# Attention on one Trainium2 core: chunk ends of the product with V, and where one query group is transposed

## The chip, the cores and the metric

The kernel runs on one core of one Trainium2 chip. The metric is the device time of one execution in microseconds (us). A core has five engines that each work through a queue of their own in order: TensorE (PE in the rows, its weight loads PEld), VectorE (DVE), ScalarE (ACT), GpSimd (POOL) and SyncE (SP, which here issues DMA transfers). They wait for one another by semaphores.

## The reference, cut to what matters

The program is an attention, then a dense layer, then a routed layer. The change touches the attention alone:

```
B, H, S, D = 4, 8, 1152, 64
q_pool = q.reshape(B, H, S // 2, 2, D).mean(axis=3)      # 576 queries a head
scores = np.matmul(q_pool, k.transpose(0, 1, 3, 2)) / np.sqrt(D)
attn = np.exp(scores - np.max(scores, axis=-1, keepdims=True))
attn = attn / (np.sum(attn, axis=-1, keepdims=True) + 1e-09)
out = np.matmul(attn, v)                                  # then the two layers
```

All arithmetic is 32 bit; the matmuls take each operand as a high part in a rounded format and a low part with the rest, so most products are issued twice or more.

## The kernel before

**Tiles and steps.** `attention` (L24) works on 16 pairs of heads. A pair has 2 × 576 = 1152 queries, which are nine tiles of 128; tile 4 holds the end of the first head and the start of the second. The main loop (L280) has one step `g` for each tile: `i, t = divmod(g, 9)` is the pair and the tile. A step works on two tiles at once: it finishes tile `g` and prepares tile `g+2`. The order of the work within a step is written out in `SEQ` (L17), and every engine gets its instructions in that order:

- `q1`, `q0` (`qk`, L158): scores of tile `g+2`, as products of the transposed queries `qa`/`qb` and the transposed keys `kst`; six matmuls of 384 columns (two into `Sb`, four into `Sa`), for tile 4 twice as many. `Sa` has one buffer in PSUM, so its next scores wait for ScalarE's exponential of the last ones.
- `m1`, `m0`, `bias` (L174 to L179): row maxima on VectorE; `e0`, `e1` (`exp`, L180): exponentials on ScalarE, into `P`.
- `t0`, `t1`, `t2` (`tp`, L212): nine transposes on TensorE of tile `g`'s `P`, three to a PSUM tile `T`; `c0` to `c2` (`evH`, L226) copy them out on ScalarE as high parts `PH`, `l0` to `l2` (`evL`, L228) subtract on VectorE for the low parts `PL`. `T` is a ring of three buffers, and everything else that is transposed takes its buffers from the same ring, in order.
- `av`, `aw` (`takeav`, L275): matmuls of the product with V, from a list that is filled chunk by chunk. `AVN[t]` is how many a step takes, the larger half at `av`, the rest at `aw`.
- `pool`, `scl`: GpSimd's work (high and low parts of keys, values and queries, from the table `POOL`; the scaling of finished outputs by `rB`, L244).
- `prep`: transposes of later pairs' queries and keys, from the table `PREP`: `T0` to `T2` are keys (`top`, L123), `q0` to `q2` query groups (`qop`, L132). Each is three transposes into a `T` and one or two copies by ScalarE; a query group then also issues two DMA transfers `qb<-qa` on SP (L145, L146).
- `inv`: reciprocals of the row sums (`invT`, L191, one transpose into a `T` at t=3 and t=7), their way through DRAM, and the load of `rB` (`invB`, L199, on SP at t=0 and t=5); `st`: stores of outputs.
- `sum`, `dec`: sums of rows, and from step 70 on single instructions that decode the next layer's weights.

**Chunks.** The product with V is made in four chunks a pair (`av_ops`, L230) of 256, 320, 320 and 256 queries. Each has 18 matmuls (nine key tiles, high and low) that add up in `O`, for which PSUM has one buffer. The last one of a chunk is followed by ScalarE's copy `xo<-O` (L242), and the first of the next chunk waits for that copy. `DONE` (L274) says after which step a chunk's matmuls are put on the list: `{1:[0],4:[1],6:[2],8:[3]}`, step and chunk. With the counts of before, a pair's chunk 2 begins at t=7 after one matmul that ends chunk 1, and chunk 3 begins at t=0 of the next pair after four matmuls that end chunk 2; chunks 0 and 3 end with the last matmul of t=4 and of t=2.

Of the kernel before, what the change touches and what calls it, by code (L numbers as in the profile page):

```python
# [14 lines left out]


SEQ='q1 q0 m1 sum dec t0 c0 m0 pool scl t1 c1 bias l0 t2 av c2 l1 e0 e1 l2 aw prep inv st'.split()  # L17
AVN=(9,3,10,7,11,7,10,7,8)
PREP={0:((1,'T0'),),2:((1,'T1'),),3:((1,'T2'),),5:((1,'q2'),),7:((2,'q0'),),8:((2,'q1'),)}
POOL={0:((0,'vH1'),(0,'vL1')),1:((1,'H0'),(1,'L0')),3:((1,'H1'),(1,'L1')),4:((1,'H2'),(1,'L2')),5:((2,'qadd'),),6:((2,'qH'),(2,'qL')),8:((1,'vH0'),(1,'vL0'))}  # L20
SPQ={4:((1,'D0'),),7:((1,'D1'),)}
SCALE=(7,8,11,12)
# [1 line left out]
def attention(tc, q, k, v, xS, rS, ident, pairs=None, extra=(), start=lambda: None):  # L24
# [5 lines left out]
    with ctx:  # L30
# [18 lines left out]
        def load(i,what="qkv",eng=None):  # L49
            if i>=len(pairs): return  # L50
            b,hp=pairs[i]; h0=2*hp
            d=D_.setdefault(i,dict(ks={},vs={},kst={}))
            for w in what:
                if w=='q':
                    t=d['qn']=ld.tile([128,KT,2,D],F32,name="qn")
                    (eng or nc.sync).dma_start(out=t,in_=q[b,h0:h0+2].rearrange("h (s r) d -> (h s) (r d)",r=2).rearrange("(t p) x -> p t x",p=128))
                else:
                    t=d[w+'n']=ld.tile([128,2,KT,D],F32,name=w+"n")
                    (eng or nc.sync).dma_start(out=t,in_={'k':k,'v':v}[w][b,h0:h0+2].rearrange("h (p t) d -> p h t d",p=128))
# [98 lines left out]
        def qk(g,n):  # L158
            i,t=divmod(g,9); d=D_[i]
            if g not in st: new(g)  # L160
            A=QA[i%2]; Bq=QB[i%2]
            if t==4: L=[(512,0),(640,1)]
            else: L=[(128*t,0)] if t<4 else [(128*t+128,1)]
            ops=[(w[:,c:c+128],h) for c,h in L for w in (A,Bq)]
            if n==0:
                o=psS.tile([128,2,512],F32,name="Sa"); st[g]['S'][0]=o[:,:,0:384]
                outs=[(o[:,j,0:384],j) for j in range(2)]
            else:
                o=psU.tile([128,384],F32,name="Sb"); st[g]['S'][1]=o
                outs=[(o,2)]  # L170
            for o,j in outs:
                for x,(w,h) in enumerate(ops):
                    nc.tensor.matmul(o,w,d['kst'][h][:,j*384:(j+1)*384],start=(x==0),stop=(x==len(ops)-1))  # L173
        def smax(g,n):  # L174
            s=st[g]
            nc.vector.tensor_reduce(out=s['nm'][:,n:n+1],in_=s['S'][n],axis=AX.XY if n==0 else AX.X,op=ALU.max,negate=True)  # L176
        def bias(g):
            nm=st[g]['nm']
            nc.vector.tensor_reduce(out=st[g]['bs'],in_=nm,axis=AX.X,op=ALU.min)  # L179
        def exp(g,n):  # L180
            s=st[g]; P=s['P']
            o=P[:,0:768].rearrange("p (c x) -> p c x",x=384) if n==0 else P[:,768:1152]
            nc.scalar.activation(out=o,in_=s['S'][n],func=AF.Exp,bias=s['bs'],scale=1.0,accum_out=s['su'][:,n:n+1])  # L183
# [3 lines left out]
        def ssum(i,h):  # L187
            a,b=TS[h]; r=inv[i,h]=sm.tile([128,2,5],F32,name="rc",bufs=2)
            nc.vector.tensor_reduce(out=r[:,0,0:b-a],in_=sus[:,i%2,a:b],axis=AX.X,op=ALU.add)
            nc.vector.reciprocal(out=r[:,1,0:b-a],in_=r[:,0,0:b-a])  # L190
        def invT(i,h):  # L191
            a,b=TS[h]; bb,hp=pairs[i]; n=b-a
            T=psT.tile([128,384],F32,name="T",tag="T")
            nc.tensor.transpose(T[0:n,0:128],inv.pop((i,h))[:,1,0:n],ident)
            o=sm.tile([5,128],F32,name="ro",bufs=1)
            nc.scalar.copy(out=o[0:n],in_=T[0:n,0:128])
            flat=rS[bb][hp:hp+1].rearrange("o h s -> (o h s)")
            nc.sync.dma_start(out=flat[128*a:128*b].rearrange("(t p) -> t p",p=128),in_=o[0:n])
        def invB(i,h):  # L199
            bb,hp=pairs[i]  # L200
            flat=rS[bb][hp:hp+1].rearrange("o h s -> (o h s)")
            r=rB[i,h]=sm.tile([128,576],F32,name="rB",bufs=2)
            nc.sync.dma_start(out=r,in_=flat[576*h:576*h+576].partition_broadcast(128))
# [8 lines left out]
        def tp(g,j):  # L212
            T=psT.tile([128,384],F32,name="T",tag="T"); P=st[g]['P']
            for n in range(3):
                kt=3*j+n
                nc.tensor.transpose(T[:,n*128:(n+1)*128],P[:,kt*128:(kt+1)*128],ident)  # L216
            st[g][j]=T
# [8 lines left out]
        def evH(g,j):  # L226
            for H,L,src in parts(g,j): nc.scalar.copy(out=H,in_=src)  # L227
        def evL(g,j):  # L228
            for H,L,src in reversed(list(parts(g,j))): nc.vector.tensor_tensor(out=L,in0=src,in1=H.bitcast(F32),op=ALU.subtract)  # L229
# [24 lines left out]
        def take(l,n=1):  # L254
            for _ in range(n):
                if l: l.pop(0)()
        ops={}
        def do(i,*names):

            if i>=N: return  # L260
            if i not in ops: ops[i]=pool_ops(i,i==0)|prep_ops(i)
            for n in names:
                o=ops[i].pop(n,None)
                if o: o()
# [10 lines left out]
        def takeav(n):  # L275
            while avq and n>0:
                avq[0].pop(0)(); n-=1
                if not avq[0]: avq.pop(0)
        stores=[]; sums={}
        for g in range(NG+4):  # L280
            i,t=divmod(g,9)
            if g<NG:
                if t==2 and i>0: load(i+1,'v')
                if t==2: load(i+2,'q')
                if t==5: load(i+2,'k')
            f2=g+2<NG; f0=g<NG
            if not f0:
                while avq: takeav(99)
            for op in SEQ:
                a=op[:-1]; n=op[-1]  # L290
                if op=='scl':
                    if g in at: x,y=at.pop(g); x(); stores.append((g,y))
                elif op=='st':
                    while stores and (stores[0][0]<g or not f0): stores.pop(0)[1]()
                elif op=='inv':
                    if f0 and t in (3,7): invT(i,t//4)
                    if t==5 and f0: invB(i,0)
                    if t==0 and i>0: invB(i-1,1)
                    for di,x in SPQ.get(t,()): f0 and do(i+di,x)
                    if g in (0,2): do(1,'q0' if g==0 else 'q1')  # L300
                elif not f0: pass
                elif a=='q': f2 and qk(g+2,int(n))
                elif a=='m': f2 and smax(g+2,int(n))
                elif a=='e': f2 and exp(g+2,int(n))
                elif op=='bias': f2 and bias(g+2)
                elif a=='t': tp(g,int(n))
                elif a=='c': evH(g,int(n))
                elif op in ('av','aw'): takeav((AVN[t]+(op=='av'))//2)
                elif a=='l': evL(g,int(n))
                elif op=='sum':  # L310
                    if t in (3,7): ssum(i,t//4)
                elif op in ('pool','prep'):
                    for di,n in (POOL if op=='pool' else PREP).get(t,()): do(i+di,n)
                elif op=='dec':
                    want=NX*max(0,g-70)//max(1,NG-74); take(extra,want-(NX-len(extra)))
                else: raise Exception(op)
            if f0:
                for c in DONE.get(t,[]): avq.append(av_ops(i,c))
# [552 lines left out]
def full(tc,q,k,v,w_in,w_out,emb,tau,w1,w2,out,dbg=None):  # L871
# [7 lines left out]
    with contextlib.ExitStack() as ctx:  # L879
# [7 lines left out]
        with tc.manual_schedule():  # L887
# [17 lines left out]
            for n in range(4):  # L905
                pre+=ops[n][1]
                if n+2<4: pre.append(ops[n+2][0])
            for n in range(2): pre+=[lambda n=n: X.load(n)]+X.split_ops(n)
            attention(tc,q,k,v,xS,rS,ident,extra=pre,start=norms)
            wp2=pool(right,"w2",side="right")  # L910
            W0.append(wp2.tile([128,2,1024],F32R,name="W2",tag="W2"))
# [109 lines left out]
```

## Time and profile before

| | us |
|---|---|
| median of 3 runs | 1350.07 (1348.87 to 1350.55) |
| profiled execution, its own time | 1348.71 |
| span of that execution, first to last instruction | 1346.6 |
| TensorE busy (its weight loads) | 1229.3 (1084.1) |
| VectorE, ScalarE, GpSimd busy | 1095.5, 892.2, 635.6 |

Times in the rows are us from the start of the span. A row of a timeline has the start, the duration, the engine, the source line, the operation, what is written and read, and how many instructions were merged (x9); in square brackets how long the engine had been idle before it, and what it waited for. The ends of matmuls are modelled, since they are pipelined: the distance of two starts says what one costs.

### The profile page before, as it was taken

What the parts mean: (1) busy time and instruction counts of PE and PEld (TensorE: products, weight loads), DVE (VectorE), ACT (ScalarE), POOL (GpSimd) and SP (SyncE); (2) the same over time, 40 slices, a digit from 0 to 9 for tenths busy, and PEclk for the clock granted to TensorE, in tenths of its full rate; (3) what the DMA queues carried; (4) which work ended last, traced back from release to release, by engine and by line L of the source; (5) the groups of instructions that cost most, each with busy time, mean ns of one, the idle gap of its engine ahead of it and who ended that gap; (6) DMA issues with size and microseconds to landing.
All of it is one profiled execution on the core that took longest, in us unless ns stands there. A gap on an engine that the chain in (4) does not pass through costs nothing. (4 is left out here: it accounts for less than half of the span.)

```text
span 1346.6 us, 22379 instructions
## 1 busy us (share of the span) xinstructions
PE 1229.3 (91%) x7341; PEld 1084.1 (81%) x7341; DVE 1095.5 (81%) x1970; ACT 892.2 (66%) x2059; POOL 635.6 (47%) x567
## 2 busy tenths in 40 slices
PE   5999999999999999977768989899999999999997
PEld 4888888888888888865657879797989887788885
DVE  5788888888888888789997697848485889998894
ACT  6888888888888888744445645454556657576772
POOL 3444444444555555256667443424342435455852
PEclk9999999999999999989898999999999999999999
DMA  5554555556555575244331311010101323258710
GB/s 165 141 143 127 128 154 138 139 142 168 152 151 137 132 187 140 58 139 117 109 102 48 109 41 36 25 40 16 40 17 47 138 72 138 94 191 328 278 36 22
DMA packets 119624, 154.34 MB, mean 115 GB/s; under 512 B 12135, under 2 KB 93943, under 8 KB 115152
## 3 DMA queue, kind: packets, MB, share of 16 engines
q1 hardware_dynamic: 115232, 140.93, 36.7%
q0 software_dynamic: 3696, 11.34, 2.4%
q8 instruction: 60, 0.98, 0.3%
q10 hardware_dynamic: 576, 0.59, 0.1%
q14 instruction: 60, 0.49, 0.1%
HBM read 155.48 MB, written 20.28 MB: 131 GB/s over the span
## 5 line engine op out<-in xcount | busy, mean ns | idle before, releaser
L430 PE MATMUL h<-xH,W 128*128 128x384 f32 (+1 forms) x896 | 229.0, 327 | 51.5 <-ACT yt L439 37.5
L227 ACT CAST PH<-T 128x384 fp32r<-128x384 f32 (+1 forms) x480 | 185.7, 460 | 84.7 <-PE T L216 84.6
L229 DVE TENSOR_TENSOR PL<-T,PH 128x384 fp32r<-128x384 f32 (+1 forms) x480 | 217.4, 508 | 6.4 <-ACT PH L227 6.3
L430 PEld LDWEIGHTS h<-xH,W 128*128 128x128 f32 x896 | 161.8, 195 | 72.3 <-ACT yt L439 48.3
L453 POOL TENSOR_TENSOR gL<-et,gH 128x384 fp32r<-128x384 f32 (+1 forms) x112 | 120.1, 1072 | 197.7 <-ACT gH L452 170.1
L818 DVE TENSOR_TENSOR W<-sg,W 128x2048 fp32r<-128x2048 f32 (+1 forms) x84 | 193.9, 2341 | 14.1 <-POOL W L816 7.2
L435 ACT ACTIVATE em<-h 128x384 f32<-128x384 f32 (+1 forms) x112 | 49.8, 445 | 224.4 <-DVE et L444 149.5
L239 PE MATMUL O<-PH,vs 128*128 128x256 f32 (+1 forms) x576 | 166.3, 311 | 17.9 <-ACT xo L242 17.9
L176 DVE TENSOR_REDUCE nm<-Sa 128x1 f32<-128x768 f32 x144 | 136.8, 950 | 40.6 <-PE Sa L173 35.1
L216 PE MATMUL T<-ident,P 128*128 128x128 f32 x1296 | 164.8, 272 | 0.0
L239 PE MATMUL O<-PL,vs 128*128 128x256 f32 (+1 forms) x576 | 161.9, 303 | 0.0
L216 PEld LDWEIGHTS T<-ident,P 128*128 128x128 f32 x1296 | 150.1, 140 | 5.2
L430 PE MATMUL h<-xL,W 128*128 128x384 f32 (+1 forms) x448 | 144.0, 321 | 0.7 <-DVE xL L385 0.7
L444 DVE SCALAR_TENSOR_TENSOR et<-em,et 128x384 f32<-128x384 f32 (+1 forms) x112 | 69.5, 621 | 84.4 <-ACT em L441 82.8
L183 ACT ACTIVATE P<-Sa,bs 128x768 f32<-128x768 f32 x144 | 133.6, 928 | 4.1 <-DVE bs L179 3.9
L173 PE MATMUL Sa<-kst,qa 128*128 128x384 f32 x320 | 114.5, 358 | 16.7 <-ACT P L183 14.8
L239 PEld LDWEIGHTS O<-PH,vs 128*128 128x128 f32 x576 | 108.6, 189 | 25.6 <-ACT xo L242 23.9
L817 ACT CAST W<-sg 128x2048 fp32r<-128x2048 f32 (+1 forms) x63 | 114.2, 1835 | 15.0 <-DMA sg<-moe_w 15.0
L461 PE MATMUL y<-W,gH 128*128 128x512 f32 x288 | 115.7, 402 | 0.0
L176 DVE TENSOR_REDUCE nm<-Sb 128x1 f32<-128x384 f32 x144 | 79.8, 554 | 42.6 <-PE Sb L173 41.7
L462 PE MATMUL y<-W,gH 128*128 128x512 f32 x288 | 113.8, 395 | 0.0
L239 PEld LDWEIGHTS O<-PL,vs 128*128 128x128 f32 x576 | 108.8, 189 | 0.0
(298 smaller groups left out, 2940.9 us busy)
## 6 DMA issues: line engine op xcount, KB each, us to landing
sg<-moe_w SPq DMA_DIRECT2D x80, 1024.0 KB
qn<-q SPq DMA_DIRECT2D x16, 576.0 KB
kn<-k SPq DMA_DIRECT2D x16, 576.0 KB
rB<-rS SPq DMA_DIRECT2D x32, 288.0 KB
vn<-v SPq DMA_DIRECT2D x15, 576.0 KB
dx<-moe_w_in SPq DMA_DIRECT2D x16, 512.0 KB
dx<-moe_w_out SPq DMA_DIRECT2D x16, 512.0 KB
qb<-qa SPq DMA_DIRECT2D x64, 96.0 KB
```

Source lines behind the costliest of these rows:

```text
L173: nc.tensor.matmul(o,w,d['kst'][h][:,j*384:(j+1)*384],start=(x==0),stop=(x==len(ops)-1))
L176: nc.vector.tensor_reduce(out=s['nm'][:,n:n+1],in_=s['S'][n],axis=AX.XY if n==0 else AX.X,op=ALU.max,negate=True)
L183: nc.scalar.activation(out=o,in_=s['S'][n],func=AF.Exp,bias=s['bs'],scale=1.0,accum_out=s['su'][:,n:n+1])
L216: nc.tensor.transpose(T[:,n*128:(n+1)*128],P[:,kt*128:(kt+1)*128],ident)
L227: for H,L,src in parts(g,j): nc.scalar.copy(out=H,in_=src)
L229: for H,L,src in reversed(list(parts(g,j))): nc.vector.tensor_tensor(out=L,in0=src,in1=H.bitcast(F32),op=ALU.subtract)
L239: nc.tensor.matmul(O[0][:,:n],vs[:,kt].rearrange("p a d -> p (a d)"),R[:,kt,:n],start=first,stop=last)
L430: nc.tensor.matmul(h[:,:N],a,b[:,k,:N],start=(n==0),stop=(n==11)); n+=1
L453: nc.gpsimd.tensor_tensor(out=gL[:,:N],in0=t_,in1=gH[:,:N].bitcast(F32),op=ALU.subtract)
L461: nc.tensor.matmul(y,gH[:,sl],wH,start=(f==0),stop=False)
L817: else: nc.scalar.copy(out=H[:,q],in_=s[:,q])
L818: (nc.gpsimd if (w,j,h) in self.pool_L else nc.vector).tensor_tensor(out=L[:,q],in0=s[:,q],in1=H[:,q].bitcast(F32),op=ALU.subtract)
```

## The change

Three tables or lines of the order are changed, and no instruction is added or dropped.

- `AVN`, the matmuls of the product with V in each step, from (9,3,10,7,11,7,10,7,8) to (6,3,9,7,11,8,10,8,10). The sum stays 72. Chunks 1 and 2 now end with the last matmul of t=6 and of t=8; chunks 0 and 3 end where they did.
- `PREP`: the second query group `q1` was transposed at t=8 for the pair after the next; it now is at t=0 for the next pair, which is one step later, ahead of the first keys `T0` of the same step.
- The start-up: pair 1's `q1` was made at step 2 and now comes with the others of t=0, in step 0.

```diff
-AVN=(9,3,10,7,11,7,10,7,8)
-PREP={0:((1,'T0'),),2:((1,'T1'),),3:((1,'T2'),),5:((1,'q2'),),7:((2,'q0'),),8:((2,'q1'),)}
+AVN=(6,3,9,7,11,8,10,8,10)
+PREP={0:((1,'q1'),(1,'T0')),2:((1,'T1'),),3:((1,'T2'),),5:((1,'q2'),),7:((2,'q0'),)}
...
-                    if g in (0,2): do(1,'q0' if g==0 else 'q1')
+                    if g==0: do(1,'q0')
```

## Rows read from the trace of the kernel before

**Rows 1.** The page: the span in 40 slices, busy tenths and granted clock.

```profile
PE   5999999999999999977768989899999999999997
PEclk9999999999999999989898999999999999999999
```

**Rows 2.** Timeline, TensorE, pairs 6 and 7: the first transposes of steps.

```profile
216.93 1.14 PE L216 MATMUL T<-ident,P 128*128 128x128 f32 x9
...
220.45 1.15 PE L216 MATMUL T<-ident,P 128*128 128x128 f32 x9
...
224.77 1.15 PE L216 MATMUL T<-ident,P 128*128 128x128 f32 x9
...
228.32 1.14 PE L216 MATMUL T<-ident,P 128*128 128x128 f32 x9
...
232.68 1.14 PE L216 MATMUL T<-ident,P 128*128 128x128 f32 x9
...
236.88 1.14 PE L216 MATMUL T<-ident,P 128*128 128x128 f32 x9
...
262.56 1.14 PE L216 MATMUL T<-ident,P 128*128 128x128 f32 x9
```

**Rows 3.** Waits, first 572 us: who waited for whom, us in total, times, longest.

```profile
PE O L239 <- ACT xo L242: 17.9, 32, 0.7
```

**Rows 4.** Timeline, all engines, step t=1 of pair 7.

```profile
233.21 1.25 ACT L227 CAST PH<-T 128x384 fp32r<-128x384 f32 x3 [0.45 <-PE T L216]
...
234.32 0.93 ACT L183 ACTIVATE P<-Sa,bs 128x768 f32<-128x768 f32 x1
...
235.39 0.44 PE L173 MATMUL Sa<-kst,qa 128*128 128x384 f32 x1 [0.51 <-ACT P L183]
```

**Rows 5.** Timeline, TensorE, steps t=6 and t=7 of pair 6.

```profile
218.06 0.31 PE L239 MATMUL O<-PH,vs 128*128 128x320 f32 x1
...
219.38 0.34 PE L173 MATMUL Sb<-kst,qa 128*128 128x384 f32 x1
...
221.35 0.39 PE L239 MATMUL O<-PL,vs 128*128 128x320 f32 x1
222.29 0.41 PE L239 MATMUL O<-PH,vs 128*128 128x320 f32 x1 [0.56 <-ACT xo L242]
...
223.28 0.49 PE L136 MATMUL T<-ident,qsp 128*128 128x128 f32 x3
```

**Rows 6.** Timeline, VectorE, step t=0 of pair 7.

```profile
229.58 1.01 DVE L229 TENSOR_TENSOR PL<-T,PH 128x384 fp32r<-128x384 f32 x2
```

**Rows 7.** Timeline, all engines, the first step of the main loop.

```profile
24.05 1.48 DVE L229 TENSOR_TENSOR PL<-T,PH 128x384 fp32r<-128x384 f32 x3
...
25.18 0.31 PEld L136 LDWEIGHTS T<-ident,qsp 128*128 128x128 f32 x3 [0.22 <-issue]
...
26.61 1.15 PE L216 MATMUL T<-ident,P 128*128 128x128 f32 x9
```

**Rows 8.** Timeline, ScalarE, ends of steps t=8 and t=0.

```profile
227.85 0.58 ACT L137 ACTIVATE qa<-T 128x256 fp32r<-128x256 f32 x2
...
232.26 0.50 ACT L129 COPY KX<-T 128x384 f32<-128x384 f32 x1
```

**Rows 9.** Timelines of SP's issues and of GpSimd, steps t=0 to t=2.

```profile
229.61 0.59 SPq L146 DMA_DIRECT2D qb<-qa  x1
...
230.88 0.45 SPq L203 DMA_DIRECT2D rB<-rS  x1
...
235.82 0.88 POOL L244 TENSOR_TENSOR xo<-xo,rB 128x320 f32<-128x320 f32 x1 [1.37 <-DMA rB<-rS]
240.83 0.51 POOL L66 TENSOR_SCALAR KH<-KX 128x384 fp32r<-128x384 f32 x1 [4.13 <-ACT KX L129]
```

**Rows 10.** Timeline, VectorE: decode instructions in t=7 and t=0, first and last of four.

```profile
323.74 0.66 DVE L346 SCALAR_TENSOR_TENSOR dx<-dx 128x512 int32<-128x512 int32 x1
...
436.17 0.42 DVE L342 TENSOR_SCALAR dx<-dx 128x512 int32<-128x512 int32 x1
```

## The prediction

> **What bounds the kernel now.** I read the forty slices first [rows 1]: TensorE stands at nine tenths and over through the first 42% of the span, which is the attention, and its granted clock is in the top tenth there, the 2.4 GHz level. The change lies in that stage alone, so I ask what sets the length of one of its steps. The starts of the nine-fold transposes mark the steps [rows 2]; from one start to the next I get, for pair 6 of 16: t=6 3.52 us, t=7 4.32, t=8 3.55, and for pair 7 t=0 4.36 and t=1 4.20. The period of a pair is 262.56 − 228.32 = 34.24 us. Two steps of nine thus stand 0.8 us above their neighbours, and t=1 is long for a reason of its own.
>
> The reason for 3.52 is a loop between TensorE and ScalarE, read at t=1 [rows 2, 4]: transposes start at 232.68, ScalarE's first copy of them at 233.21, its exponential of the tile two steps on at 234.32, and only then may TensorE overwrite that tile's scores, at 235.39: 2.71 us. At t=1 eight score matmuls follow (236.88 − 235.39 = 1.49) and make 4.20; a usual tile has four, and the loop is about 3.5, where t=6 and t=8 already stand. A step cannot be shorter than that loop, whatever TensorE saves in it.
>
> The two long steps are then read in the waits [rows 3]: the product with V waits for ScalarE's copy `xo` 32 times, 17.9 us in all, that is twice a pair. The place is seen at t=7 [rows 5]: one product matmul at 221.35, which ends a chunk, then nothing until 222.29, because the only buffer `O` has to be copied out before the next chunk may begin in it. At t=0, by the counts, the wait falls after the fourth product matmul.
>
> **The change part by part.**
>
> *Chunk ends.* With the new counts the chunks end with the last product of t=6, t=8, t=2 and t=4: 8+10, 8+10, 6+3+9, 7+11, each 18. The copy of `O` then runs behind the step's two exponentials, while TensorE does scores and nine transposes, and the next chunk starts 0.90 us after the next transposes do (221.35 − 220.45), 3.52 + 0.90 = 4.42 into the step that ended the chunk [rows 2, 5]. ScalarE is done with its exponentials 3.08 into a step, and a copy takes about 0.5 (as that of the keys) [rows 2, 8]: `O` is free at 3.6. So the wait is gone unless ScalarE comes 0.8 us late.
>
> Step t=7 afterwards: ten products of 320 columns and all before them end at 219.38 − 216.93 = 2.45 us into t=6; nine of those intervals are 219.38 − 218.06 = 1.32, so 0.147 each [rows 2, 5]. t=7 will have eight: 2.45 − 2×0.147 = 2.16. What follows (second prep transpose group, the row of reciprocals, six score matmuls) took 224.77 − 223.28 = 1.49. Sum 3.65, above the loop, so TensorE bounds it. Gain 4.32 − 3.65 = 0.67; it cannot be more than 0.80, to the loop. The Trainium skill, "TensorE: Matmul & The Clock Gate", section "Wait — 56ns, not 53.3ns?", gives N ÷ 2.4 GHz + 2.5 ns between matmuls, 136 ns for 320 columns; by it t=7 would come to about 3.57, by estimate, and the change gain 1 us more in all. The row says 0.147, and the row is used.
>
> *Other counts.* t=8 gets ten products and no prep, which is what t=6 is now: 3.55 to 3.52, gain 0.03. t=5 gets eight and keeps its prep, which is what t=8 is now: from the loop's 3.51 to 3.55, a loss of 0.04 (nothing, if it is longer today). t=2 has one product less in a step that already stands near the loop: nothing, at best 0.12.
>
> *Second query group moved to t=0.* All that it issues counts. On TensorE three transposes, beside three fewer products. On PSUM: the ring `T` has three buffers taken in order, so in t=0 the query group takes the buffer of that step's first transposes and the keys take that of the second; the keys wait until VectorE's second subtraction is through. That ends at 229.58 + 1.01 = 230.59, or 2.27 into t=0 [rows 2, 6]. The trace has this very pattern once, in the start-up step: subtractions from 24.05, the second prep group's weights at 25.18, that is 0.12 after the second subtraction (24.05 + 1.01), and the next step's transposes at 26.61, 1.43 later [rows 7]. So t=0 becomes 2.27 + 0.12 + 1.43 = 3.82: it does not fall to the loop, and gains 4.36 − 3.82 = 0.54. Bounds: 0.85 if the wait doesn't bind (the loop, 3.51), and 0.24 if the keys come another 0.3 late.
>
> On ScalarE, the two `qa` copies and the key copy now stand in a row at the end of t=0. The first starts 227.85 − 224.77 = 3.08 after a step's start, the two take 0.58, the key copy 0.50 [rows 2, 8]: free at 4.16, and the next step wants ScalarE at 3.82 + 0.53 = 4.35. Hidden, with 0.2 to spare; if that cover goes, each 0.1 costs 0.1 a pair at t=1, which is bound by the loop. On SP, the two `qb` transfers now go ahead of the load of `rB`, at about 3.66 (the copies' end) + 2 × 0.6 = 4.9 into t=0 instead of 230.88 − 228.32 = 2.56 [rows 2, 9]. GpSimd's scaling waits for `rB`; with t=0 shorter by 0.54 it would come 2.3 + 0.5, some 2.9 us, later against the steps; behind it GpSimd idles 4.13 before the next key copy [rows 9]. Hidden, with 1.2 to spare.
>
> *Evacuation.* The copy of `O` leaves later than it could, behind the exponentials. The Trainium skill, "PSUM — Partial Sum Buffer", section "Summary: rules for kernel authors", says to evacuate promptly, which speaks against this order. By the rows nobody wants `O` until the next step's 0.90, so I charge nothing.
>
> *Start-up and decode.* In pair 0 three prep groups now meet in one step: +0.4 there, −0.3 where the second query group stood, nothing in sum. The decode instructions on VectorE that fall into t=7 and t=0 lie today beside the stall: the first takes 0.66, the last 0.42, four in all [rows 10]. Without the stall I let most of that show: 4 × 0.4, say 1.5 us lost.
>
> *Sum.* t=7: 16 × 0.67 = 10.7. t=0: 15 × 0.54 = 8.1 (pair 0 has no chunk before it). t=8 against t=5: nothing. Less 1.5: 17.3 us. The profiled execution took 1348.71 (span 1346.6, some 2 us around it): 1331.4. The median of the three runs is 1.4 above the profiled one, so I name 1332.8. The stages behind the attention start when its last step ends, and I carry the gain over one to one, with 2 us of doubt.
>
> **The rivals.**
>
> *Everything to the loop.* The keys don't wait in t=0 and TensorE keeps pace in t=7: 16 × 0.80 + 15 × 0.85 − 1.5 = 24, so 1326. For it: TensorE's own work in t=0 is small. Against: the ring has three buffers, and the start-up step shows the wait.
>
> *Only t=7 pays.* If the prep groups get their buffers one subtraction later each, the keys wait for the third, 229.58 + 1.48 = 231.06, and t=0 is 2.74 + 0.12 + 1.43 = 4.29: gain 0.07. Then 10.7 + 1.0 − 1.5 = 10.2, so 1340. Against: the start-up step again [rows 7].
>
> *The wait stays.* The Trainium skill, "Perfetto Trace Analysis", section "Matmuls", wants independent groups in different PSUM banks so that the copy of one overlaps the next group. Here `O` stays one buffer. As a mechanism of this kernel: the copy of `O` queues behind the exponentials and the first product waits at the start of a step instead of in its middle, with the same 17.9 us [rows 3]. Time 1350. Against: the 0.8 us that lie between, above.
>
> *Slower.* The load of `rB` behind the two `qb` transfers. From its issue to its use 235.82 − 230.88 = 4.94 us pass now; the room is 1.2. If in the new place it took over 6.1, GpSimd's key copies would slip, and with them the keys that SP spreads for the next pair; taking no slack there, every further microsecond costs 15 us. From 7.3 the gain is gone; at 8 the time would be 1350.1 − 17.3 + 1.9 × 15 = 1361. Against: the transfer is the same, and no byte is added to the stage.
>
> **How the numbers follow.** The forecast has 0.68, everything to the loop 0.12, only t=7 0.13, the wait stays 0.04, slower 0.03. The predicted time is 1332.8. The range takes in the forecast's bounds (t=0 alone 15 × 0.3 either way) and both neighbours: 1325 to 1341. About 0.2% (2.7 us) is what a measurement of this kernel can tell from no change. Faster by more than that are the first three cases: 0.93; the same 0.04; slower 0.03.
>
> **What would show it.** Right: no wait of the product for `xo` within the attention but in its last drain; steps of 3.65 at t=7 and 3.8 at t=0; a period of 33.0 us instead of 34.24; in t=0 the keys' transposes start 2.4 after the step and wait for VectorE; ScalarE's first copy of t=1 still 0.53 behind its transposes. t=0 at 3.5 or at 4.3 would say that I have the ring wrong. t=1 above 4.20 would say that ScalarE's three copies in a row are not covered. Scalings waiting for `rB`, with key copies on GpSimd no longer idle before them, would say that SP's order costs. If the attention ends 17 us earlier but the kernel doesn't, a transfer or a decode behind it had its own due time.

## The result, and the profile after

The changed kernel takes 1334.38 us (median of 4 runs, 1332.78 to 1335.27) against 1350.31 for the kernel before, run beside it: a ratio of 0.9877, 95% interval 0.9865 to 0.989. Twice more it was run beside the experiments below, at 1331.6 against 1350.35 (0.9863, 0.9846 to 0.9879) and 1331.81 against 1350.48 (0.986, 0.9845 to 0.9875). The gain is thus 16 to 19 us; 17.3 was forecast. The profiled execution of after took 1335.27 (span 1333.4).

The page of after, its span in 40 slices and the granted clock, answers to [rows 1]:

```profile
PE   5999999999999999877778989999999999999996
PEclk9999999999999999999989999999999999999999
```

The attention has the same nines and the same clock; what changed is seen only from step to step. The timeline of TensorE, first transposes of steps from t=6 of pair 6 to t=2 of pair 7, and t=0 of pair 8; this answers to [rows 2]:

```profile
245.06 1.15 PE L216 MATMUL T<-ident,P 128*128 128x128 f32 x9
...
248.58 1.14 PE L216 MATMUL T<-ident,P 128*128 128x128 f32 x9
...
252.22 1.14 PE L216 MATMUL T<-ident,P 128*128 128x128 f32 x9
...
255.74 1.15 PE L216 MATMUL T<-ident,P 128*128 128x128 f32 x9
...
259.52 1.14 PE L216 MATMUL T<-ident,P 128*128 128x128 f32 x9
...
263.72 1.04 PE L216 MATMUL T<-ident,P 128*128 128x128 f32 x8
...
288.68 1.15 PE L216 MATMUL T<-ident,P 128*128 128x128 f32 x9
```

| step | before | forecast | after |
|---|---|---|---|
| t=6 | 3.52 | 3.52 | 248.58 − 245.06 = 3.52 |
| t=7 | 4.32 | 3.65 | 252.22 − 248.58 = 3.64 |
| t=8 | 3.55 | 3.52 | 255.74 − 252.22 = 3.52 |
| t=0 | 4.36 | 3.82 | 259.52 − 255.74 = 3.78 |
| t=1 | 4.20 | 4.20 | 263.72 − 259.52 = 4.20 |
| pair | 34.24 | 33.0 | 288.68 − 255.74 = 32.94 |

The waits of the first 555 us (who waited for whom, us in total, times, longest), beside [rows 3]:

```profile
POOL xo L244 <- DMA rB<-rS: 67.7, 22, 4.5
...
PEld T L128 <- DVE PL L229: 3.2, 16, 0.6
...
ACT KX L129 <- DMA kst<-KX: 0.9, 1, 0.9
...
PE O L239 <- ACT xo L242: 0.6, 1, 0.6
```

Of the product's 32 waits for `xo` one is left, in the drain behind the start of the last step. What came in their place is small: the keys' transposes wait for VectorE 16 times, as forecast, and GpSimd's scaling waits longer for `rB`, which nobody feels. The third line is a wait that the forecast did not name; it is taken up below.

How t=0 of pair 7 runs now, TensorE's timeline, beside [rows 7]:

```profile
257.60 0.55 PE L136 MATMUL T<-ident,qsp 128*128 128x128 f32 x3
258.07 0.55 PE L128 MATMUL T<-ident,kn 128*128 128x128 f32 x3
```

The query group starts 257.60 − 255.74 = 1.86 into the step, when the first buffer of `T` is free, and the keys at 2.33, when the second is (forecast 2.39); the next step's transposes come 259.52 − 258.07 = 1.45 later (forecast 1.43).

How the copy of `O` fits in, ScalarE and TensorE at the end of t=8 of pair 6 and the start of t=0:

```profile
255.31 0.45 ACT L242 COPY xo<-O 128x320 f32<-128x320 f32 x1
...
256.64 0.37 PE L239 MATMUL O<-PH,vs 128*128 128x256 f32 x1
```

The copy ends at 255.76, 3.54 into t=8 (forecast 3.6), and the first product of the next chunk starts 0.88 later.

### The profile page after: what moved, and what is told of

It reads as the page before. It is cut to its first block, busy times and chain, and to the rows that moved or that the text cites. A ratio compares the mean times of both kernels' runs of the same rounds, so it can differ in the third digit from the quotient of the medians.

```text
span 1333.4 us, 22357 instructions
## 1 busy us (share of the span) xinstructions
PE 1227.6 (92%) x7341; PEld 1082.5 (81%) x7341; DVE 1096.5 (82%) x1970; ACT 890.2 (67%) x2059; POOL 634.9 (48%) x567
## 5 line engine op out<-in xcount | busy, mean ns | idle before, releaser
L227 ACT CAST PH<-T 128x384 fp32r<-128x384 f32 (+1 forms) x480 | 182.8, 460 | 74.3 <-PE T L216 73.7
L239 PE MATMUL O<-PL,vs 128*128 128x256 f32 (+1 forms) x576 | 158.5, 299 | 0.0
L444 DVE SCALAR_TENSOR_TENSOR et<-em,et 128x384 f32<-128x384 f32 (+1 forms) x112 | 69.2, 618 | 84.8 <-ACT em L441 79.9
L173 PE MATMUL Sa<-kst,qb 128*128 128x384 f32 x320 | 108.1, 338 | 0.0
```

The costliest lines, as they stand in the source:

```text
L239: nc.tensor.matmul(O[0][:,:n],vs[:,kt].rearrange("p a d -> p (a d)"),R[:,kt,:n],start=first,stop=last)
```

## The experiments

**The new counts alone, and the new place alone.** The change has two parts, and each was run by itself.

```diff
 # ends_alone: the kernel before with
-AVN=(9,3,10,7,11,7,10,7,8)
+AVN=(6,3,9,7,11,8,10,8,10)
 # query_alone: the changed kernel with the old counts
-AVN=(6,3,9,7,11,8,10,8,10)
+AVN=(9,3,10,7,11,7,10,7,8)
```

> The new counts alone; the second query group stays at t=8. If the two waits at the chunk ends were the cost: t=7 goes from 4.33 to 3.65 as in the changed kernel, t=0 (six products, only the keys prepared) falls to the loop, 3.51, and t=8 carries ten products and a prep group, 3.52 + 0.3 = 3.8. A pair 34.24 to 33.0, total about 1332. If the place of the query group makes the gain: t=7 and t=0 stay near 4.3, total 1350.

Measured: 1331.73 (1330.69 to 1332.69), ratio 0.9862 (0.9846 to 0.9879). In its trace t=7 is 3.64, t=0 3.52, t=8 3.82, a regular pair 32.98.

> The query group moved to t=0, with the counts of before. If the chunk ends were the cost, both waits for the copy of O are still there (32 of them, some 18 us); t=0 has 0.25 to 0.3 more transposes, 4.38 to 4.65; t=8 falls to 3.51. Total 1350 + 15 x 0.25 + 0.9 of start-up = 1355. If the move makes the gain: 1335 or less.

Measured: 1355.63 (1353.25 to 1356.4), ratio 1.0036 (1.0023 to 1.0048), slower. The waits of its first 572 us (two more of them come later, since its attention ends later), and t=0 of pair 6 in TensorE's timeline:

```profile
PE O L239 <- ACT xo L242: 16.6, 30, 0.6
```

```profile
230.16 1.14 PE L216 MATMUL T<-ident,P 128*128 128x128 f32 x9
...
232.45 0.39 PE L239 MATMUL O<-PH,vs 128*128 128x256 f32 x1 [0.56 <-ACT xo L242]
...
233.14 0.49 PE L136 MATMUL T<-ident,qsp 128*128 128x128 f32 x3
233.47 0.49 PE L128 MATMUL T<-ident,kn 128*128 128x128 f32 x3
...
234.87 1.14 PE L216 MATMUL T<-ident,P 128*128 128x128 f32 x9
```

The wait stands where it stood, and t=0 is 234.87 − 230.16 = 4.71: the transposes are added to it. So the counts make the whole gain. Under the new counts the move of the query group takes 0.3 off t=8, where ten products and a prep group would meet (3.82 to 3.52), and puts 0.24 on t=0 (3.52 to 3.76): a regular pair is 32.94 with the move and 32.98 without, and the totals, 1334.38 to 1331.6 and 1331.73, cannot be told apart.

**One matmul over the line.**

```diff
 # one_over: the changed kernel with
-AVN=(6,3,9,7,11,8,10,8,10)
+AVN=(6,3,9,7,11,8,9,9,10)
```

> The changed kernel with one product matmul a pair moved over a chunk end: nine at t=6 and nine at t=7, so that chunk 1 ends with the first product of t=7. If the wait for the copy of O is the cost, it comes back 16 times and t=7 goes from 3.64 to 4.6 (two products more than the 4.32 it had with seven): 16 x 0.97 = 15.5 us, total 1350. If only the spread of TensorE's load over the steps counts, one matmul costs 0.15 at t=7 and nothing at t=6: 16 x 0.15 = 2.4 us, total 1337.

Measured: 1345.15 (1344.31 to 1347.58), ratio 0.9963 (0.9952 to 0.9975). TensorE's timeline at t=7 of pair 6, up to t=8:

```profile
254.20 1.14 PE L216 MATMUL T<-ident,P 128*128 128x128 f32 x9
...
256.05 0.42 PE L239 MATMUL O<-PH,vs 128*128 128x320 f32 x1 [0.56 <-ACT xo L242]
...
258.82 0.38 PE L216 MATMUL T<-ident,P 128*128 128x128 f32 x2
```

t=7 is 258.82 − 254.20 = 4.62, as expected, and every other step is as in the changed kernel. One matmul a pair, moved over a chunk end, costs 0.98 a pair where its own work is 0.15. That is the chunk end shown apart from the spread of the work. The total was expected at 1350 and came at 1345; beside the 1331.6 to 1334.4 of the changed kernel it is 11 to 14 us more, where 16 × 0.98 would make 15.7. Summed over its trace t=7 is 14.6 above the changed kernel's first profile, since five of the 16 pairs pay less than 0.98.

**Half of the products.** This run asks what holds the other steps at 3.5. It leaves out the products with the low parts `PL`; the parts themselves are still made.

```diff
 # half_products: the changed kernel with
-AVN=(6,3,9,7,11,8,10,8,10)
+AVN=(3,2,4,4,5,4,5,4,5)
...
-ops.append(mm(kt,PH,kt==0,False)); ops.append(mm(kt,PL,False,kt==KT-1))
+ops.append(mm(kt,PH,kt==0,kt==KT-1))
```

> Left out: the low parts of the product with V, so half of its matmuls; chunks still end with a step. 36 matmuls of 0.117 to 0.147 a pair are 4.8 us of TensorE, 76 us in all. If the loop with ScalarE and the ring of T set the steps: t=0 stays 3.76, t=1 4.21, t=4 3.70, the others stay 3.51 and t=7 falls from 3.64 to 3.53 at most; total 1331 or 1332. If TensorE's work sets them, a pair falls by several us and the total towards 1260.

Measured: 1328.7 (1327.41 to 1329.59). Run beside it, the changed kernel took 1331.6. Half of the product, some 76 us of TensorE's work, is worth 3 us. TensorE's timeline from t=5 of pair 6 to t=1 of pair 7:

```profile
239.07 1.14 PE L216 MATMUL T<-ident,P 128*128 128x128 f32 x9
...
242.60 1.14 PE L216 MATMUL T<-ident,P 128*128 128x128 f32 x9
...
245.31 0.45 PE L173 MATMUL Sa<-kst,qa 128*128 128x384 f32 x1 [0.49 <-ACT P L183]
...
246.13 1.14 PE L216 MATMUL T<-ident,P 128*128 128x128 f32 x9
...
249.65 1.15 PE L216 MATMUL T<-ident,P 128*128 128x128 f32 x9
...
253.17 1.14 PE L216 MATMUL T<-ident,P 128*128 128x128 f32 x9
...
256.93 1.14 PE L216 MATMUL T<-ident,P 128*128 128x128 f32 x9
```

The steps are 3.53, 3.53, 3.52, 3.52 and, at t=0, 3.76. With half the products TensorE stands idle for 0.49 at t=6, waiting for ScalarE's exponential, and the step is no shorter. The loop of transposes, ScalarE's copies, exponential and next scores is the floor, and t=0 stays above it with half the products: it is held by the ring `T`, not by what TensorE has to do.

**The query group elsewhere, first try.**

```diff
 # query_t1: the changed kernel with
-PREP={0:((1,'q1'),(1,'T0')),2:((1,'T1'),),3:((1,'T2'),),5:((1,'q2'),),7:((2,'q0'),)}
+PREP={0:((1,'T0'),),1:((1,'q1'),),2:((1,'T1'),),3:((1,'T2'),),5:((1,'q2'),),7:((2,'q0'),)}
```

> The changed kernel with the second query group at t=1, where TensorE waits for ScalarE anyway. If t=0 stands at 3.76 because the keys' transposes wait for a buffer of T: t=0 falls to the loop, 3.51 (15 x 0.25 = 3.75 us), t=1 stays 4.21, the start-up step loses its third prep group (1.2 us): total 1329.5. If t=0 is long because of something else: 3.76 stays. A price that may show: the key copy at t=0 then comes 0.6 us earlier and may wait longer for the transfers that still read KX; then t=1 grows, by up to 0.6 a pair, and the total is up to 1338.

Measured: 1333.16 (1332.66 to 1334.51), ratio 0.9871 (0.9854 to 0.9887). t=0 did fall to 3.52, which says once more what had held it. But t=1 grew, by two things. TensorE's timeline, t=1 of pair 7 (from 260.90) to t=2:

```profile
260.90 1.27 PE L216 MATMUL T<-ident,P 128*128 128x128 f32 x9
...
262.77 0.55 PE L136 MATMUL T<-ident,qsp 128*128 128x128 f32 x3 [0.24 <-DVE PL L229]
...
265.27 1.15 PE L216 MATMUL T<-ident,P 128*128 128x128 f32 x9
```

In the step with few products the query group itself waits for VectorE, 1.87 into the step, and the twelve score matmuls stand behind it: 4.37 instead of 4.21, and 4.34 or more in every pair but the last. And in several pairs t=1 is longer still, up to 5.52, since the key copy waits for transfers (six such waits, 4.2 us). Summed over the attention, t=0 gave 3.6 us and t=1 took 4.3. My expectation had the second price and not the first.

**The wait for the keys' transfers.** The changed kernel has single pairs with a longer t=1. The keys of the next pair are spread from `KH` and `KX` into `kst` by two groups of four transfers on SP, `D0` and `D1` (table `SPQ`), and `KX` has one buffer. All engines, end of t=0 and t=1 of pair 5 in its first profile:

```profile
193.02 0.82 PE L216 MATMUL T<-ident,P 128*128 128x128 f32 x6
...
193.78 0.48 ACT L129 COPY KX<-T 128x384 f32<-128x384 f32 x1 [0.85 <-DMA kst<-KX]
...
194.31 0.55 PE L216 MATMUL T<-ident,P 128*128 128x128 f32 x3 [0.47 <-ACT KX L129]
```

ScalarE's copy into `KX` waits 0.85 for the transfers that still read the last pair's `KX` (D1, sent out at t=7); the third buffer of `T` comes free late, the transposes stop after six of nine, and the step is 4.84. To test it, D1 goes out a step earlier; the changed kernel was run beside it.

```diff
 # after_again, after_third: the changed kernel as it is
 # after_d1: the changed kernel with
-SPQ={4:((1,'D0'),),7:((1,'D1'),)}
+SPQ={4:((1,'D0'),),6:((1,'D1'),)}
```

> The changed kernel once more, for comparison with the others of this call: 1334, steps as in its first profile. If the longer t=1 of single pairs (4.30, 4.84, 4.40, 4.58, 4.48) comes from a landing that varies, other pairs or other sizes show it now; if it comes from the order of the work, the same pairs show it.

Measured: 1331.6. t=1 is 4.67, 4.86 and 4.72 in pairs 3, 5 and 13, the same three as in the first profile (4.30, 4.84, 4.48).

> The changed kernel with the second half of the next pair's keys sent out (D1, the transfers that read KX) at t=6 instead of t=7. If t=1 is longer in single pairs because the key copy of t=0 waits for those transfers to land, then nearly all pairs have 4.21 at t=1 (those with a decode instruction apart), 1 to 1.5 us less than the changed kernel, total about 1333. If ScalarE's three copies in a row make it, t=1 is as in the changed kernel.

Measured: 1331.91 (1331.27 to 1333.6), no difference in the total that could be told. But t=1 is 4.23, 4.21 and 4.21 in those three pairs, and no wait of the key copy is left in its trace. In the changed kernel's own traces one wait a profile is put down to the transfers and nearly all of the others to TensorE; that they all go when D1 goes out earlier says that they were the same wait. Only 4.37 remains in three pairs with a decode instruction. The wait is shown, and so is its size: t=1 sums to 67.9 here and to 69.1, 69.5 and 69.2 in the three profiles of the changed kernel, so 1.2 to 1.6 us in all. Why it is those three pairs stays open.

**The query group elsewhere, second try.**

```diff
 # query_t4_d1: after_d1 with
-PREP={0:((1,'q1'),(1,'T0')),2:((1,'T1'),),3:((1,'T2'),),5:((1,'q2'),),7:((2,'q0'),)}
+PREP={0:((1,'T0'),),4:((1,'q1'),),2:((1,'T1'),),3:((1,'T2'),),5:((1,'q2'),),7:((2,'q0'),)}
```

> As the one before, and the second query group at t=4, alone in its step with a loop of 3.70. By the ring of T and the loop: t=0 falls from 3.76 to 3.52, t=4 grows by 0.07 at most to 3.77, t=1 stays 4.21 though the key copy comes earlier, since the transfers have landed. A pair 32.93 to 32.75, with the waits gone 4 us less than the changed kernel: 1330. If the place of the query group is indifferent: 1334.

Measured: 1345.16 (1344.05 to 1345.76), ratio 0.9964 (0.9952 to 0.9977). t=0 is 3.52, t=4 3.70 and t=1 4.22, all as hoped, but t=6 went from 3.52 to between 4.2 and 5.8. SP's issues for t=4 of pair 6, which leave while TensorE is in t=5 and t=6 (these start at 245.27 and 248.80), then TensorE at the end of t=6:

```profile
245.72 0.47 SPq L145 DMA_DIRECT2D qb<-qa  x1
246.24 0.59 SPq L146 DMA_DIRECT2D qb<-qa  x1
246.94 1.94 SPq L106 DMA_DIRECT2D kst<-KH  x1
248.98 0.61 SPq L106 DMA_DIRECT2D kst<-KX  x1
249.64 0.62 SPq L106 DMA_DIRECT2D kst<-KH  x1
250.32 0.62 SPq L106 DMA_DIRECT2D kst<-KX  x1
```

```profile
253.48 0.41 PE L173 MATMUL Sb<-kst,qa 128*128 128x384 f32 x1 [2.06 <-DMA kst<-KX]
```

The query group's two transfers wait on SP for ScalarE's copies, and the next pair's first keys (D0) wait behind them: the last leaves at 250.32, and TensorE, which wants those keys at t=7, stands for 2.06. I had counted the query group's engines and left out what its transfers pass on SP. This is the mechanism that the prediction gave to its slower rival, in another place.

> The second query group at t=4 and D1 at t=6 as in query_t4_d1, but at t=4 the keys' transfers D0 go out on SP ahead of the query group's two. If t=6 grew there because the next pair's keys landed late behind those two: t=6 is 3.52 again, t=0 3.52, t=1 4.21, t=4 3.70; a pair 32.7, total about 1328 to 1329, less than the changed kernel. If t=6 grew because of the query group's other work or of D1 at t=6, it stays at 4.2 to 5.8 and the total at 1345.

```diff
 # query_t4_keys_first: query_t4_d1 with the keys' transfers issued ahead of the prep
-                    for di,x in SPQ.get(t,()): f0 and do(i+di,x)
...
                 elif op in ('pool','prep'):
+                    for di,x in SPQ.get(t,()) if op=='prep' else (): do(i+di,x)
```

Measured: 1327.35 (1325.69 to 1329.44), ratio 0.9831 (0.9818 to 0.9845) to the kernel before. t=6 is 3.52 again, so the order on SP was the cause, and this version beats both kernels. TensorE's timeline, t=0 and t=1 of pair 6, up to t=2:

```profile
220.21 1.14 PE L216 MATMUL T<-ident,P 128*128 128x128 f32 x9
...
223.73 1.14 PE L216 MATMUL T<-ident,P 128*128 128x128 f32 x9
...
227.95 1.14 PE L216 MATMUL T<-ident,P 128*128 128x128 f32 x9
```

t=0 is 3.52 and t=1 4.22; a regular pair is 32.69 and stands at the loop everywhere but at t=7.

> The changed kernel, for comparison with the other of this call: 1331 to 1335, a pair 32.93.

Measured: 1331.81 (1330.55 to 1333.87), so the version with the query group at t=4 is some 4.5 us below the changed kernel that was run beside it.

## Why the prediction was right, and where it was off

- *The loop bounds a step* [rows 2, 4]: right; that the product is not what bounds it is shown by leaving out half of it. This carried the whole forecast, because it says what is late next once the wait for `O` is gone.
- *`O` is free 0.8 us before it is wanted*: right, 0.88 measured. One wait of 32 is left. That the copy leaves later than it could costs nothing, as charged.
- *t=7*: forecast 3.65, measured 3.64. Summed over the attention the step gave 9.8 us of the 10.7, since the first and the two last pairs gain less, and in pairs 8 and 10 a decode instruction shows (4.11 and 3.85).
- *t=0*: forecast 3.82, measured 3.76 to 3.78 in regular pairs. The wait for the second buffer of `T` was read rightly from the start-up step [rows 7]. The 15 steps gave 9.1 us, where 8.1 was forecast; both rivals about the ring (3.5 and 4.3) fell with that number. The prediction entered this gain under the move of the query group. The run with the new counts alone shows that it is the counts' (4.38 to 3.52), and that the move takes 0.24 of it back.
- *Decode*: forecast 1.5 us lost. Pairs 8 to 12 stood 3.3 us above five regular pairs before and 4.6 to 5.6 after, in three profiles: 1.3 to 2.3. The size was right, in part by luck: the four instructions at t=7 and t=0 that the forecast named cost 0.46, 0.20, 0.23 and nothing in the first profile, 0.9 in all, and the rest comes in other steps and differs from profile to profile.
- *ScalarE's three copies are covered*: as put, right, for t=1 is 4.20 and ScalarE's next copy stands 0.5 behind its transposes in regular pairs. But the step that failed is there: I counted when ScalarE is free for the key copy and not what the copy itself must wait for. The stalls that the change takes out had covered the transfers that read `KX`; without them t=1 took 1.5 us back. Three copies in a row are not needed for it: with the new counts alone, where only the key copy stands at the end of t=0, t=1 took 1.9 back. A wait of this kind was nowhere in the sum.
- *The load of `rB` goes later on SP*: GpSimd was forecast 1.2 us of slack before its next key copy, from 4.13 [rows 9]. After, the timeline of GpSimd has

```profile
264.95 0.88 POOL L244 TENSOR_TENSOR xo<-xo,rB 128x320 f32<-128x320 f32 x1 [3.48 <-DMA rB<-rS]
267.68 0.52 POOL L66 TENSOR_SCALAR KH<-KX 128x384 fp32r<-128x384 f32 x1 [1.85 <-ACT KX L129]
```

  1.85 us, where 1.2 was forecast: the cover was real, and more than half of it is used up. The slower rival stayed away here, and came when the next pair's first keys stood in that queue instead of `rB`.
- *Start-up*: forecast at nothing; in the first profile t=0 of pair 0 took 5.07 instead of 3.82, of which t=2 gave 0.35 back. In the third it took 4.24, and there the forecast holds. See the last section.
- *One to one to the end*: the attention's last step started 16.8 us earlier (567.8 to 551.0), and the span is 13.2 shorter in that profile. Two more profiles of the same kernel have 15.2 and 14.5 for the span, and the medians 16 to 19. Behind the start of the last step the span has 779 us before and 782, 779 and 781 in the three profiles after, so what lies between is within what executions differ; no stage behind was found to hold the gain back.
- *The sum*: in the first profile the steps of the attention add up to 9.8 (t=7) + 9.1 (t=0 of 15 pairs) + 0.6 (t=2) − 1.5 (t=1) − 1.2 (t=0 of pair 0) = 16.8, and the others to nothing. That this lies so near 17.3 is partly luck: 0.9 too much at t=7 stands against 1.0 too little at t=0, and the loss at t=1 was not in the sum.

## What to carry to other kernels

When an accumulator has one buffer, put the end of each group where the tensor engine has other work anyway, at the end of a software-pipelined step; here one matmul on the wrong side of that line cost a microsecond a pair, and half of all matmuls of that kind cost next to nothing. Before pricing such a wait away, find the loop that holds the neighbouring steps, since it is the floor of the gain. A stall that is removed was also cover: list the transfers that were landing under it, and for a step that is moved list what stands behind its transfers in the queue that issues them.

## What the runs showed of the hardware that I had not expected

The granted clock of the main loop's first step was not the same in executions of one program. In windows from 22.7 to 27.0 us (busy time and count of PE, PEld, DVE, ACT and POOL, then granted clock, DMA share and GB/s), the first profile of after and the third have

```profile
22.70:27.00 4.30, 3.78 (x21) 3.38 (x20) 2.51 (x5) 3.53 (x11) 0.00 (x1) 0.60 0.00 0
```

```profile
22.70:27.00 4.30, 3.49 (x26) 2.99 (x25) 2.95 (x6) 3.65 (x11) 0.06 (x1) 1.00 0.00 0
```

With 0.60, between the levels of 1.2 and 2.4 GHz, t=0 of pair 0 took 5.07 us (4.75 in the second profile, which has 0.60 too), with 1.00 it took 4.24, which is the +0.4 that the prediction had worked out. Ahead of that step TensorE had just stood idle for 2.1 us, waiting for ScalarE, in the first profile as in the kernel before, whose step had 1.00. So 0.5 to 0.8 us of the start-up come and go between executions and belong to no edit.
